# A fused attention and SwiGLU program whose order, engines and buffers stand in three tables: all three tables replaced

## The chip, the core and the metric

The program runs on one core of one Trainium2 chip. Its time is device microseconds (us), the median of three runs. The engines are PE (TensorE, matrix products), DVE (VectorE), ACT (ScalarE), POOL (GpSimd) and SP (SyncE, which here only issues DMAs). Each takes its instructions in the order in which the program holds them, and waits on semaphores for the others.

## The reference

Causal attention over 4 batches, 8 heads, 768 positions and 64 dimensions, in which heads 0, 2 and 6 see all earlier keys and the other five only the first 4 keys and a window of 64. Its output, as 3072 tokens of 512, goes through a SwiGLU block with 1536 hidden columns.

```python
scores = scale * np.matmul(q, k.transpose(0, 1, 3, 2))
stream_keep = causal & (is_sink | in_win)
mask = np.where(retr[0, :, 0, 0, None, None], full_mask, stream_mask)
scores = np.where(mask[None, :, :, :], scores, -1000000000.0)
scores = scores - np.max(scores, axis=-1, keepdims=True)
a = np.exp(scores)
a = a / (np.sum(a, axis=-1, keepdims=True) + 1e-09)
attn_out = np.matmul(a, v)
x = attn_out.transpose(0, 2, 1, 3).reshape(B * S, H * D)
g = x @ w_gate
silu = g * (1.0 / (1.0 + np.exp(-g)))
val = x @ w_val
out = silu * val @ w_out
```

## The kernel before

The work is cut into some 1060 **tasks**, and a task has a name by which the texts below call it. The 24 tiles of 128 queries (two to a pair, 12 pairs, numbered in the order of `TILES`) and the six groups of four tiles (512 tokens) of the SwiGLU block are the two counts on which names are built.

- `load q3`, `load k3`, `load x3`: DMAs of a pair's queries, keys and values, issued by SP (lines 349 and 354). `load g0`, `v0`, `o0` and so on are the sixths of the three weight matrices, 512 KB each (lines 360 and 362). They land in 11 `raw` buffers. `cq`, `ck`, `cx` and `wc` are the casts from there to 16 bits (lines 206, 208 and 212: the same copy on ACT, on POOL or DVE, and DVE's other form).
- `trq`, `trk` on PE and `evq`, `evk` turn the first five pairs' queries and keys (lines 473 and 208/206); from pair 5 on DMA transposes do it (`dq`, `dk`, line 463).
- `sc7.0` is the first unit of tile 7's scores on PE (line 567, up to eight products over 64 rows), `ex7.0` its exponentials on ACT (line 579), `mask7.0` the product with a 0/1 mask on DVE or POOL (line 587; unit 0 has 1024 columns, unit 1 has 640), `val7.1` and `val7.0` the products with the values on PE (line 597), `nm7` the division on DVE (a RECIPROCAL at line 604 and a TENSOR_TENSOR into `xb` at line 605). `sk` and `sv` are small copies of the first keys and values into later tiles' places.
- `xtr`, `xe` (tiles 0 to 7) or `xdma` (a DMA transpose by SP, line 615) put the tile's result into `xt`, the transposed input of its group.
- `gate2.8.0` and `vals2.8.0` are group 2's products for hidden block 8 (four matmuls each, line 759); `tanh` on ACT (line 765), `stt1` (line 769) and `stt2` (line 775) on DVE make the hidden activations `h_sb`. Group 0's first four blocks are halved, and the half's first column ends the name (0 or 256).
- The output projection of groups 0 to 4 uses seven products in place of eight: `out1.p1` to `out1.p7` on PE (line 839, twelve matmuls each), fed by sums of activations `hs` (line 826) and of weights `ws` (line 412) and gathered by `oe1.c11`, `oe1.r6` and so on, nearly all on DVE (line 855). Group 5 is projected plainly (`out5.0.0` and on, line 793). `st` are the stores.

PSUM has eight banks. A score unit or a tile's values take two neighbouring ones, a gate, vals or out product one, and PE may only write a bank when the reader of what stood there before (`ex`, `nm`, `stt1`, `stt2`, `oe`) is done.

No scheduler decides anything at run time or at build time. `ORDER` lists the tasks, two base-62 digits each, and the program is emitted in that order, so that each engine's queue is the list's part that falls to it; entries from 3700 up are fillers, some matmuls that keep PE going. `WAYS` has a digit for each task, the engine among those allowed, and `SLOTS` a digit for each buffer or bank that a task takes. `Plan.order` reads them:

Of the kernel before, what the change touches and what calls it, by code (L numbers as in the profile page):

```python
# [13 lines left out]


ORDER = (
    "0306071W091U1V1X000A08xy1c0D0C01050B1d1e040gy01f1gzJ1i1h2021282922232B1j1r1s021p1q1w0F2C2D2E2F1b"
    "2A2L2M2N2O2X2f2g0m1Y1a1Z1t1u1v1k0h252h1l1m2W2c242G2H2I2d2e2l2m2i2j0G271n1o1y1z3C262P2Q2R0z2t3031"
    "2J0y8e8o2n2K102U2o2p3I3J2V8t8j8m8u8v8k8l8n1x2k8f8g8p8q2x382y8h8i118r8s8w8x138y8z9893909495999A33"
    "340n9D9E0E2Z3K3D3L3M3N149B9C9F969G9H972a9192322b2Y2q2r2s2u3R3S3W3X0k1C9c9d9e9h9i9j3U3V3O2z353P36"  # L20
    "39370q1D9f9g9k9l3T3b3i3n3o3f3g0H3H3E3F2v2w0i169I9J9K9N9O9P0o179L9Q9R9M0l1F3Q3Y3Z3c3j3a0I3u40410j"
    "193k3h9m9n9o3l3m3A3B9S9T9U9r9s9t3d3e9X0J3v4344453G3p3q3r0r1G9u9p9v429Y9Z3s3t0x1H2S4647494A4H0p1A"
    "9V9WB74N4O4Q4R0K3z9q9zA10N4c3x4BB4B5B6B8Ak4K4L4V4b4C4D3yAT484M0w0sAQARASAU9a9b9y0t1E0W6K2TAlAmAV"
    "AWAX151M1O1N1PAYAZBEAfAgAhB9BABB4a0u181Q1R1SBCBDAp0v1BBFBGA0AaAbAnAoAc3wBHBIAdAe0L0M0PB20T12A41I"
    "1J1K0S4d4P0O4Z4h4g4Y4e4f5D5L5K0RAzB0B1AqArB31L0YALAM0ZAN4E4F4G4J4I6J1TAuAvAOAPAw9wA2A69xA3A7A55C"
    "5I5JAA4l4m4i4j4kACA8A9ABAD4n4v51524y53AiAj5f5lAEBMAGAFAK4S4z504T4W4UAxAy5g5nAsAtBL4q4r4o4p54BO0c"
    "AHAIAJ4s554t4u4x4wBJBKBQ56575T5U6MBNBP5W5c5XBb5j0X58595A5B707S7T6xBVBW6wBRBS5i5VBXBYBc6z5YBZBaBd"
    "5p5qBT5s605t5u4XBsBtBuCeCbCcCdCfCMCNCOCCBvBwCDCE0V6I5v0Q5F5G5H6v5k5o5M5N5O0UBiBjBk5rCPCQBlBm5E5Z"
    "5a5b5d5wCHCICJCWCXCY5m63696A666768Bh5h73CKCLC7C8C9710eCRCS5P5Q5R6465CACBCTBUC2C36y7Q6P74BnBo5x5y"
    "5z610a72CZCaBp5S625e6H6NBqBrC46B6C6F6D6GCFCGCiBeBfBgBxByBz7O7UC0C1C5C681CUCVCjCl6E6U6V6W6X6Y6R6S"  # L30
    "6T6eDmDjDkDlDnDoDpDqDrDs0b7P7X7WDtDuDv6Z6aCgChCn6b6c6d6fDUDVDWDXDY7576776g7C7D7E7F7G7L0dDwDxCkCm"
    "DSDFDGDHDPDQDRDT7b7c7d6QDADBDCDyDzE0DDDE7H80D5D6D7CsCt6O6n6o6h6i6j6kE1E27V7I7J7M7K7ND8D96l6m7879"
    "7A7BCoCpCrCuCv897Y7Z6p6q8786DKDLDMDZDaDb6L6r6s6t6uDcDdDeDfDgCwCx7e7f7R7j7m7n7o7p7q7rDNDOCyCzD0D4"
    "EhEiEjErEsEcEd88EkElEtCqD1D2D3EuEvEeDhDi7a7g7h7k7iFLFMFNFOFP7x8D8E8A8I8B8C8F8JFJFGFHFIFKFBFCFDDI"
    "DJE5E77s7t8GFEFFEp7u7v7y7w8HEXEYEZ0f838485EmEnEoEqEfEg8NEw8Y8ZE6E88T8U8VEzExEyF0EBE3E9E4EAECEDF6"
    "828K8L8M8OF1F2F3F9EFEG8Q8R8S8W8XEVEHEIEJF7F8FA7l8P7z8a8b8cEaEbESETEUEWEEEOELEM8dGiGMGTGUEKGCENER"
    "G7GVGWGjGkGJGKEPGREQFTFVGXGLGOGPGEGFGNGQG9F4GAGSGGGYGbGZF5GaGcGBGDFSGHFpFqFrFQFRG4G5GdGeFzFUFeFW"
    "FXGIG6G0G8FcFdGfFfFuFvFYFaFbGgGhG1G2G3FsFtFxGlGmFZFwFyFlFiFjFmFnFgFhFkFoGnGoGpGsGtGuGvGwGqGrGxGy"
    "GzH0H2H3H4H5H7H1H6H8H9"
)  # L40
WAYS = (
    "000010000000000000000000000000000000000000000000000000000000221202202202212200200111000111110010"
    "222200001100000000000000220022122022001011000000000000001100212002000011001001000001000001001000"
    "000201021120001000001001000000010010000010000000002221220000000000010000002000100100000020000221"
    "000000000100000002000010010000000000020200000010000000000000110000011000000100100000020001000000"
    "002202200220000000000000000012000100100000000201120000000000000000010002202202010000001001000001"
    "200000000000011002021000000000000000000200000000000000000000000000000000000000000000000000000000"
    "000000000000000000000000000000000000000000001000000000000000000000000000000000000000000000000000"
    "000000000000000000000000000000001000000010000000000000000000000000000000000000000000000000000000"
    "000000000000000000001110100011000000000001000000000000000000000000000000000000000000000000000000"  # L50
    "000000001111000001100000000000100000000000000000000000000000000000000000000000000000000000000111"
    "101100110000000000011000000000000000000000000000000000000000000000000000000000000000010000100000"
    "00000010"
)
# [965 lines left out]
```

## Time and profile before

| what | us |
| --- | --- |
| device time, median of 3 runs | 246.05 (245.79 to 246.59) |
| span of the profiled execution, first to last instruction | 244.4 |
| PE, DVE, ACT, POOL busy in it | 234.5, 186.7, 148.5, 129.0 |
| PE waiting for another engine or a DMA, longest in one place | 1.4 |

The profile gives no device time of its own for the profiled execution, only its span; the median of the three runs lies 1.65 us above that span. The profile is one execution. In its rows a number in square brackets behind an instruction is the idle time of its engine ahead of it, with who ended it; "x12" is a count; pieces of the chain of waits have a start and a duration, in us from the span's start.

### The profile page before, as it was taken

Reading aid. Unit: us, or ns where it says so; the run is one execution under the profiler, and the core shown is the slowest. Engines: PE = TensorE matmul, PEld = TensorE weight load, DVE = VectorE, ACT = ScalarE, POOL = GpSimd, SP = SyncE. Lnnn points to the kernel's source line nnn. Section 1 sums busy time; section 2 is a strip of 40 time slices with the busy share of each in tenths; the row PEclk is TensorE's granted clock in tenths of the full one; section 3 lists DMA queues with packets and bytes.
Section 4 is the critical chain, followed back from the end, with each engine's and each line's share of the span. In section 5 each row is a group of like instructions: output and inputs, shape, how many; then the busy total and the mean of one; then the engine's idle time right before and its main releaser. Section 6 shows DMA issues by size and latency. Waiting matters only on the chain.

```text
span 244.4 us, 5604 instructions
## 1 busy us (share of the span) xinstructions
PE 234.5 (96%) x2189; PEld 143.6 (59%) x2189; DVE 186.7 (76%) x324; ACT 148.5 (61%) x235; POOL 129.0 (53%) x140
## 2 busy tenths in 40 slices
...
GB/s 187 355 348 353 323 352 366 313 362 305 206 131 78 287 165 289 191 268 192 89 130 130 97 120 38 90 36 234 38 4 0 46 21 115 59 0 1 7 203 136
DMA packets 66794, 40.73 MB, mean 167 GB/s; under 512 B 25168, under 2 KB 60240, under 8 KB 66768
## 3 DMA queue, kind: packets, MB, share of 16 engines
...
q14 instruction: 9, 0.07, 0.1%
...
## 4 chain that ended last, share of the span: by engine, by line
PE 54%; DVE 19%; issue 8%; DMA 6%; POOL 5%; SPq 5%; ACT 2%; DVEq 0%; POOLq 0%
PE banks L759 34%; PE banks L839 10%; PE banks L793 4%; DMA raw<-in_moe_w_val_dram 4%; DVE h_sb L775 4%; PE banks L567 3%; DVE h_sb L826 3%; SPq L349 3%; DVE sil L769 3%; PE banks L597 2%; POOL hs_sb L826 2%; DVE out_sb L855 2%; DVE xb L605 2%; DMA xt<-xb 2%; DVE e L587 2%
## 5 line engine op out<-in xcount | busy, mean ns | idle before, releaser
L759 PE MATMUL banks<-xt,wg_sb 128*128 128x512 f16 (+1 forms) x304 | 70.3, 368 | 1.9 <-DMA xt<-xb 1.4
L759 PE MATMUL banks<-xt,wv_sb 128*128 128x512 f16 (+1 forms) x304 | 70.4, 368 | 0.8 <-DVE sil L769 0.7
L579 ACT ACTIVATE e<-banks 128x1024 f16<-128x1024 f32 (+2 forms) x68 | 58.7, 910 | 20.0 <-PE banks L567 11.7
L765 ACT ACTIVATE sig<-banks 128x512 f32<-128x512 f32 (+1 forms) x76 | 43.0, 577 | 43.5 <-PE banks L759 37.5
L769 DVE SCALAR_TENSOR_TENSOR sil<-sig,banks 128x512 f32<-128x512 f32 (+1 forms) x76 | 49.0, 656 | 14.8 <-ACT sig L765 12.6
L775 DVE SCALAR_TENSOR_TENSOR h_sb<-sil,banks 128x512 f16<-128x512 f32 (+1 forms) x76 | 48.7, 656 | 6.7 <-PE banks L759 4.4
L587 POOL TENSOR_TENSOR e<-e,m 128x640 f16<-128x640 f16 (+1 forms) x22 | 37.8, 1727 | 27.2 <-ACT e L579 24.3
L759 PEld LDWEIGHTS <-wg_sb 128*128 128x128 f16 x304 | 28.5, 98 | 30.7 <-issue 3.1
L759 PEld LDWEIGHTS <-wv_sb 128*128 128x128 f16 x304 | 28.2, 98 | 29.5 <-issue 1.2
L839 PEld LDWEIGHTS <-h_sb 128*128 128x128 f16 x360 | 34.8, 98 | 7.9 <-issue 0.7
L826 POOL TENSOR_TENSOR hs_sb<-h_sb 128x768 f16<-128x768 f16 x7 | 11.5, 1640 | 40.9 <-DVE h_sb L775 29.4
L855 DVE TENSOR_TENSOR out_sb<-banks,out_sb 128x512 f32<-128x512 f32 x35 | 23.6, 685 | 4.7 <-PE banks L839 4.4
L826 POOL TENSOR_TENSOR h_sb<-h_sb 128x768 f16<-128x768 f16 x11 | 18.0, 1639 | 8.2 <-PE banks L839 4.4
L839 PE MATMUL banks<-wo_sb,h_sb 128*128 128x256 f16 x180 | 21.9, 273 | 0.0
L839 PE MATMUL banks<-wt_sb,h_sb 128*128 128x256 f16 x180 | 21.5, 273 | 0.4 <-DVE out_sb L855 0.4
L567 PE MATMUL banks<-qT,kT 64*128 64x128 f16 x472 | 20.6, 218 | 1.1 <-DVE xb L605 1.0
L567 PEld LDWEIGHTS <-kT 64*128 64x128 f16 x472 | 14.6, 94 | 11.0 <-issue 10.2
L597 PEld LDWEIGHTS <-e 128*128 128x128 f16 x472 | 17.1, 97 | 4.3 <-ACT vt L206 0.9
L597 PE MATMUL banks<-vt,e 128*128 128x65 f16 x472 | 18.2, 193 | 1.0 <-POOL vt L208 0.7
L605 DVE TENSOR_TENSOR xb<-banks,rc 128x512 f16<-128x512 f32 x24 | 16.6, 691 | 0.8
L208 POOL CAST vt<-raw 64x512 f16<-64x512 f32 x22 | 14.4, 654 | 4.8 <-DMA raw<-in_v_dram 2.3
L206 ACT COPY out_sb<-banks 128x512 f32<-128x512 f32 (+1 forms) x7 | 4.0, 570 | 19.1 <-PE banks L793 16.0
...
## 6 DMA issues: line engine op xcount, KB each, us to landing
...
```

What stands on the lines that cost most here:

```text
L567: nc.tensor.matmul(sc[:, c:c + n, :], weights, moving, start=first, stop=last)
L579: nc.scalar.activation(out=to, in_=src, func=AF.Exp, scale=scale)
L587: ENG[task().way].tensor_tensor(out=ev, in0=ev, in1=mm, op=ALU.mult)
L597: nc.tensor.matmul(avs[t][:, odd, n * 66:n * 66 + 65], ee, vv, start=(m == 0), stop=(m == len(bl) - 1))
L605: nc.vector.tensor_tensor(out=xb.rearrange("p n o d -> p o n d"), in0=av[:, :, :, 0:64], in1=rc.to_broadcast([128, 2, 4, 64]), op=ALU.mult)
L759: nc.tensor.matmul(ps, wsb[:, kk, j * 128:(j + 1) * 128], xt[:, kk, c[0]:c[1]], start=(kk == 0), stop=(kk == 3))
L765: nc.scalar.activation(out=sg[g, j, c], in_=gs[g, j, c], func=AF.Tanh, scale=0.5)
L769: nc.vector.scalar_tensor_tensor(out=sl[g, j, c], in0=sg.pop((g, j, c)), scalar=1.0, op0=ALU.add, in1=gs.pop((g, j, c)), op1=ALU.mult)
L775: nc.vector.scalar_tensor_tensor(out=hs[g, j][:, c[0]:c[1]], in0=sl.pop((g, j, c)), scalar=0.5, op0=ALU.mult, in1=vs.pop((g, j, c)), op1=A ...
L826: ENG[T_hs[g, x][part].way].tensor_tensor(out=to, in0=a, in1=b, op=op)
L839: nc.tensor.matmul(rooms[g, p][:, x], left[:, j, 128 * x:128 * x + 128], right[:, j], start=(j == 0), stop=(j == NK - 1))
L855: nc.vector.tensor_tensor(out=cell(*to), in0=rooms[g, p], in1=cell(*other), op=ALU.add)
```

## The change

Only the three tables differ. Every task, its arithmetic and its shapes are the same, and so is the number of fillers (11 matmuls in three places, placed differently). The first line of each table, before and after:

```diff
 ORDER = (
-    "0306071W091U1V1X000A08xy1c0D0C01050B1d1e040gy01f1gzJ1i1h2021282922232B1j1r1s021p1q1w0F2C2D2E2F1b"
+    "060207xl0009030A08011U1V0D041W1X0C1c1f1dyE0B1g201h1i210g1e2822231j1r05292B0m1s1p0h2C1a2A1Z2D2E0E"
...
 WAYS = (
-    "000010000000000000000000000000000000000000000000000000000000221202202212202200200111000111110010"
+    "000010000000000000000000000000000000000000000000000000000000222222002202222220011011011110111012"
...
 SLOTS = (
-    "0014237653916A152371476981504A39A2564807049A28352A9168410016041002241601230163620442561014104122"
+    "101423105745851125376045A37912261A7446230143026693A470201012001302241602011043423044540401320063"
```

Decoded, the engines of these tasks change (tasks of a kind on ACT / DVE / POOL):

| kind | before | after |
| --- | --- | --- |
| casts of queries and keys, `cq` `ck` | 12 / 3 / 13 | 8 / 4 / 16 |
| casts of values, `cx` | 16 / 10 / 22 | 15 / 7 / 26 |
| first keys and values, `sk` `sv` | 14 / 8 / 10 | 7 / 7 / 18 |
| weights, `wc` | 6 / 2 / 12 | 5 / 1 / 14 |
| masks | - / 16 / 22 | - / 20 / 18 |
| sums, `hs` and `ws` | - / 23 / 29 | - / 21 / 31 |

On PE, scores stand in 31 separate runs where they stood in 32. Three places of the new order follow.

**SP, around the transposes of group 2's input.** These are SP's rows around the DMA transposes of tiles 10, 11 and 9 into the `xt` of group 2 (line 615; `xb_1598` is tile 10, `xb_1695` tile 11, `xb_1517` tile 9; line 354 are loads, 861 a store). Before:

```order
L463 DMA_TRANSPOSE kT0_104<-hq_1526 128x8x64
L354 DMA raw_1555<-in_v_dram 128x8x128
L861 DMA out_0_dram<-out_sb_94 128x2x512
L615 DMA_TRANSPOSE xt_1343<-xb_1598 128x4x128
L354 DMA raw_1665<-in_q_dram 128x8x128
L615 DMA_TRANSPOSE xt_1343<-xb_1695 128x4x128
L615 DMA_TRANSPOSE xt_1343<-xb_1517 128x4x128
L354 DMA raw_1831<-in_k_dram 128x8x128
```

And now, where `xb_1615` is tile 10, `xb_1382` tile 9 and `xb_1731` tile 11:

```order
L463 DMA_TRANSPOSE qT0_106<-hq_1465 128x8x64
L861 DMA out_0_dram<-out_sb_94 128x2x512
L463 DMA_TRANSPOSE qT1_107<-hq_1378 128x8x64
L615 DMA_TRANSPOSE xt_1421<-xb_1615 128x4x128
L354 DMA raw_1659<-in_v_dram 128x8x128
L615 DMA_TRANSPOSE xt_1421<-xb_1382 128x4x128
L615 DMA_TRANSPOSE xt_1421<-xb_1731 128x4x128
L354 DMA raw_1750<-in_q_dram 128x8x128
```

Tile 9 moved ahead of tile 11, which comes last; the load in front of tile 11's transpose is now one ahead of both.

**DVE, between the norms of tiles 3 and 5.** DVE's rows in the first gates of group 0 (L769 is `stt1`, L775 `stt2`, both in halves here; L587 a mask). Before:

```order
L775 SCALAR_TENSOR_TENSOR h_sb_92<-sil_534,banks_87 128x256
L769 SCALAR_TENSOR_TENSOR sil_542<-sig_540,banks_87 128x256
L769 SCALAR_TENSOR_TENSOR sil_546<-sig_544,banks_87 128x256
L212 TENSOR_REDUCE kT0_104<-kT0_104 128x2x2x2
L212 TENSOR_REDUCE kT0_104<-kT0_104 64x2x2
L775 SCALAR_TENSOR_TENSOR h_sb_92<-sil_542,banks_87 128x256
L775 SCALAR_TENSOR_TENSOR h_sb_92<-sil_546,banks_87 128x256
L775 SCALAR_TENSOR_TENSOR h_sb_92<-sil_530,banks_87 128x256
```

And now:

```order
L775 SCALAR_TENSOR_TENSOR h_sb_92<-sil_509,banks_87 128x256
L587 TENSOR_TENSOR e_468<-e_468,m1_102 128x1024
L769 SCALAR_TENSOR_TENSOR sil_583<-sig_572,banks_87 128x256
L769 SCALAR_TENSOR_TENSOR sil_589<-sig_566,banks_87 128x256
L775 SCALAR_TENSOR_TENSOR h_sb_92<-sil_542,banks_87 128x256
L769 SCALAR_TENSOR_TENSOR sil_610<-sig_593,banks_87 128x256
L775 SCALAR_TENSOR_TENSOR h_sb_92<-sil_583,banks_87 128x256
L587 TENSOR_TENSOR e_517<-e_517,m2_103 128x640
```

Masks of tiles 4 to 7, of which seven of eight stood in POOL's queue, are now all in DVE's.

**DVE, at the norm of tile 16.** L826 is a sum `hs` for group 2, L604 and L605 the norm. Before:

```order
L769 SCALAR_TENSOR_TENSOR sil_2212<-sig_2210,banks_87 128x512
L826 TENSOR_TENSOR h_sb_92<-hs_sb_93,h_sb_92 128x3x256
L604 RECIPROCAL rc_2259<-banks_87 128x8
L605 TENSOR_TENSOR xb_2258<-banks_87,rc_2259 128x2x4x64
L769 SCALAR_TENSOR_TENSOR sil_2270<-sig_2268,banks_87 128x512
```

And now:

```order
L769 SCALAR_TENSOR_TENSOR sil_2203<-sig_2196,banks_87 128x512
L604 RECIPROCAL rc_2227<-banks_87 128x8
L605 TENSOR_TENSOR xb_2226<-banks_87,rc_2227 128x2x4x64
L769 SCALAR_TENSOR_TENSOR sil_2242<-sig_2237,banks_87 128x512
L775 SCALAR_TENSOR_TENSOR h_sb_92<-sil_2203,banks_87 128x512
L769 SCALAR_TENSOR_TENSOR sil_2261<-sig_2256,banks_87 128x512
L769 SCALAR_TENSOR_TENSOR sil_2305<-sig_2301,banks_87 128x512
L212 TENSOR_REDUCE kT1_105<-kT1_105 128x2x2x2
L212 TENSOR_REDUCE kT1_105<-kT1_105 64x2x2
L826 TENSOR_TENSOR h_sb_92<-hs_sb_93,h_sb_92 128x3x256
```

The sum stood just ahead of the norm and stands eight rows behind it.

More of the change, by code (lines that the diff above doesn't have):

```diff
@@ L22 @@
[L22 to L36, printed above, removed]
@@ L37 @@
-    "G7GVGWGjGkGJGKEPGREQFTFVGXGLGOGPGEGFGNGQG9F4GAGSGGGYGbGZF5GaGcGBGDFSGHFpFqFrFQFRG4G5GdGeFzFUFeFW"
-    "FXGIG6G0G8FcFdGfFfFuFvFYFaFbGgGhG1G2G3FsFtFxGlGmFZFwFyFlFiFjFmFnFgFhFkFoGnGoGpGsGtGuGvGwGqGrGxGy"
-    "GzH0H2H3H4H5H7H1H6H8H9"
+    "060207xl0009030A08011U1V0D041W1X0C1c1f1dyE0B1g201h1i210g1e2822231j1r05292B0m1s1p0h2C1a2A1Z2D2E0E"
+    "1q1Y2X2L2F1b1w2f2M2W2N2g1t2O2h0F1u2S1k1l2c1v2425yG0n262d1m0G2G2H272e2l2I2i2m0z1n1y1o2P0y2Q1z2j0k"
+    "2J2t2R8o112o308p2K2p2U1x8q0q8r312V8e102x8f33138g8j340H2b8t8m0i388s8u9D8k2k2y3C988l8h8v0o998w8i2Y"
@@ new lines @@
+    "3I149A938n2Z0l328y949B3D958z963J8x9G900j9E3L2n1C97913M9C2q922r3K0I2a9c2s3N2u3R9F9d3W2z9h0v3X1D3S"
+    "9H359e369i3U3O0J37399k3P3b3F9j9f3V169l0p3H3i3l3E3f173j9N9g0r3g3Q2v9I3T9O3k3Y0x191F2w3Z9P9Q0s2T0t"
+    "3u9L9R9J3a9m3m0w3h400M9n9X9o0u3v3d9K9Y3n9S3c3G3o0K9M419r1A3e42439Z9T1B3p3q9s9U0P449a3r45469b1G49"
+    "3s4H123A9V9t4A3t9u3B479WB99v15484N4C4KBA9p4D0TBB1I4Q9qAQ4R0N1E4OBCAuAR1M0Q1H4L1NAV181J3yAfBD0L4P"
+    "ATAg9z3wAhAi0R3xASAzAWAj4Z9wA10W4BAv4MAxAUA3AX4E0S4FB4AwB01KB1B2B50O4G1QAY4YB3AL9y5G4eA44bAM4c1L"
@@ new lines @@
+    "B64hAkAyA0AZ4gBEAlAN9xAO1R4f3z1O4IAnBF5g0XAP5h4S4T0YA21TAa5DA5ApBG5f5L1S4UA84W5lAm1PAA4VA9Aq4JAo"
+    "4lAr4i5nAs4j4vAB4aAC5CAt5KA76v4mB75JA6ADAb4q540bBHAc555o4k4rAE4dBI5IB86w4o514yAF4pAH4n52BLAGAd53"
+    "AIAK4sAJAe4t4z5mBZ4uBM4x5W565T5k5XBOBJ0Z4w575c4XBNBRBK505UBP5859BQ5i5VBVBU5H5ABX5BBW5j0U5Y5v5MBY"
+    "Bb0c5NBS0V5EBa5w745p5sBTBcCM5t0eCbCN5u0a5F6MBdCH5O6H5q5ZCO5aCKCICcCJ6z6OBs5dCLCPBtCd606ICeBu5rCQ"
+    "Bv6PCfBi5b6QBw6366Bj6981646NBkBl67CC65Bm6E5P5x5Q5y6A5RBnCD5SC2BoCE68Be735z616Z6UBh6aCF5e6VBf6BCG"
@@ new lines @@
+    "6C7S62BxBp6FC36DC00fBy6J70Bz6G6X6R7PC4C56S0dC16WCW71C6C76y7W6TBqC86YC9CA72CXBrCRCY7O7XCZCS6x6KCT"
+    "CU88CiCBDjCa6bCVDkDmCkDl6cDo6d6eCjDyDp6g7TDqCgDzDn7UClE07F7C75ChBg7GDP7VCmD5DQ76DRE17LD6DrCn777D"
+    "E2DtDs6LDwD7857RDuDADv7ECsDBDxDC7b6k6hCt7c80DD6l7H78DUDE6i7I8479DX7ADV6f7JDWDK6jDYD8DL7KDeDM6m6n"
+    "6pD97Y866qDS836oCo7QDT897M7d6rDf7NCp6s7ZDF7j6t7B7aDNDgDGDH6uDZDO7e7p7m7qCw7f7nDI7g7oCu7hCvCyCrDJ"
+    "CxErCzE6EcD07iD4FGEd7xDaEeDcCqDbEsEuDdFH82Dh7kEt7r8G7s7lDi8HF1EvE887FID1F27tF38DE58A8ID28BF4FJ8N"
@@ L40 @@
+    "F58C8E7u7v8JFB7wE78Y8TFKFC7zEa8ZFD8U7yD3EXE38FEYEZ8KE48LFE8M8OEBEA8PFFESECE98Q8W8V8REDEFET8XEhEG"
+    "8SEUEVEbFL8aFM8bEiFNF98cEfEW8dEmEjEJEgEnEwELFOF6FPEoEpF7ExF8EzEqG4FAEkG5GHElEEEHG6FTGJEyEIFuGKF0"
+    "GCFvEKGEFVEMG7GLFxGFG8FwEOENFSERGMG9GNEPFQGAEQGBGdFzGeFRGfFYFyFUGOFXFWGgGPGQGRGDG0FaFpGSG2FZFbGh"
+    "FcG1G3FqGWFdFiFrGGGTGYGUGVFlFeFsFfGlFjFmGiGIFnFgGjGXGZFtGbGkGaGnGmGoGcFhGpFkGsGqFoGtGrGuGxGvGyGw"
+    "GzH2H0H3H1H4H7H5H6H8H9"
 )
 WAYS = (
-    "000010000000000000000000000000000000000000000000000000000000221202202202212200200111000111110010"
@@ L43 @@
[L43 to L52, printed above, removed]
@@ L53 @@
-    "00000010"
+    "000010000000000000000000000000000000000000000000000000000000222222002202222220011011011110111012"
+    "122101101100000000000000110022122022010011000000000000001200222221000011000000000001100000000000"
+    "001100221210000000000000000000001000000000000000002200200000000010000000000000000000000220002102"
+    "000000000000000001100000010000000000221000000000000000001000010002022000000100000000100001000000"
+    "002102020000000001001000000011000100100000000122220000000100000010010000202222000000001001000001"
@@ new lines @@
+    "200010010000010022222000000010000000000210001000000000000000000000000000000000000000000000000000"
+    "000000000000000000000000000000000000000000101001001100000000000010000000000000000000000000000000"
+    "000000000000000000000000000000001000000110000000000000000000000000000000000000000000000000000000"
+    "000000000000000000001111100011000000000000000000000000000000000000000000000000000000000000000000"
+    "000000001011100001000000000000100000000000000000000000000000000000000000000000000000000000000000"
@@ L54 @@
+    "001000110000000000001000000000000000000000000000000000000000000000000000000000000000110001100000"
+    "00000001"
 )
 SLOTS = (
-    "0014237653916A152371476981504A39A2564807049A28352A9168410016041002241601230163620442561014104122"
-    "636011642065221025144416322211256461406003404624344620616540610143626540604164236062324342142254"
-    "041614064616325426212246140636104325614261306242452460436460636014122636230644521206164434062601"
-    "020211341120003102001134000210400214105510131201001011040122021303213020111113411111040020200051"
```

13 lines of the change are left out of this document (6 added, 7 removed).

## The prediction

> **What bounds the kernel now.** I read the page's busy times first:
>
> ```profile
> span 244.4 us, 5604 instructions
> ...
> PE 234.5 (96%) x2189; PEld 143.6 (59%) x2189; DVE 186.7 (76%) x324; ACT 148.5 (61%) x235; POOL 129.0 (53%) x140
> ```
>
> PE is not busy for 9.9 us of the span. To see whether its busy time is work or hides slow stretches, I took the last stage out of the chain of waits (start, duration, what):
>
> ```profile
> 200.24 13.81 PE banks L759 x64
> ...
> 227.06 3.93 PE banks L839 x36
> 230.99 10.40 PE banks L793 x60
> ```
>
> 64 gate and vals matmuls in 13.81 us are 0.216 us each, a gate or vals task (four) 0.86; an `out` product of twelve is 1.31. PE runs without a gap here, and nothing in the tables can shorten these matmuls. **PE is the bound**, so the change can win only what PE waits. The timeline of PE shows where (idle time ahead in brackets, and who ended it):
>
> ```profile
> 1.36 4.69 PE L321 MATMUL banks<-ident 128*128 128x512 f16 x12 [1.36 <-POOL ident L234]
> ...
> 17.75 0.42 PE L597 MATMUL banks<-vt,e 128*128 128x65 f16 x8 [0.71 <-POOL vt L208]
> ...
> 56.59 1.02 PE L759 MATMUL banks<-xt,wg_sb 128*128 128x512 f16 x4 [0.45 <-DVE sil L769]
> ...
> 59.60 1.02 PE L759 MATMUL banks<-xt,wv_sb 128*128 128x512 f16 x4 [0.25 <-DVE sil L769]
> ...
> 82.35 1.47 PE L839 MATMUL banks<-wt_sb,hs_sb 128*128 128x256 f16 x12 [0.18 <-DVE out_sb L855]
> ...
> 91.00 0.83 PE L567 MATMUL banks<-qT,kT 64*128 64x128 f16 x22 [0.44 <-DVE xb L605]
> ...
> 136.75 0.85 PE L567 MATMUL banks<-qT,kT 64*128 64x128 f16 x24 [0.51 <-DVE xb L605]
> ...
> 188.95 1.47 PE L839 MATMUL banks<-wt_sb,h_sb 128*128 128x256 f16 x12 [0.45 <-DVE out_sb L855]
> ...
> 191.40 1.02 PE L759 MATMUL banks<-xt,wv_sb 128*128 128x512 f16 x4 [0.43 <-DVE sil L769]
> ```
>
> and PE's waits by who ended them have one more, the longest:
>
> ```profile
> PE banks L759 <- DMA xt<-xb: 1.4, 1, 1.4
> ```
>
> 1.36 us come before the first matmul and about 3.0 after the last (230.99 + 10.40 = 241.4); the other 5.5 are spread in small waits, most of them ended by DVE. That is the whole prize, 2% of the time. Beyond PE, DVE is close behind in the middle, as the windows view shows (PE, PEld, DVE, ACT and POOL busy, in us):
>
> ```profile
> 21.00:49.00 28.00, 27.87 (x328) 18.50 (x326) 23.00 (x50) 25.82 (x46) 26.93 (x28) 1.00 1.10 341
> 56.00:98.00 42.00, 40.58 (x394) 27.32 (x393) 40.72 (x68) 32.40 (x48) 24.75 (x22) 1.00 0.91 204
> ```
>
> DVE works 40.72 of 42 us between 56 and 98; between 21 and 49 it has 5 us to spare, and POOL 1.
>
> **The change part by part.** The sum is made on the span and carried to the median: 246.05 plus the difference. Differences within 0.3% (0.74 us) count as no change; about that much is what measuring this kernel can tell.
>
> *One score run fewer: -0.2.* A run of scores pays at its ends beyond its matmuls:
>
> ```profile
> 24.11 0.33 PE banks L567 x8
> ...
> 111.92 0.77 PE banks L567 x22
> ```
>
> Eight in 0.33 and 22 in 0.77 give 0.031 each and 0.08 at the entry; the exit isn't shown, and I allow 0 to 0.3.
>
> *The start: -0.5.* The 0.71 us wait at 17.75, for a value cast, sits behind exponentials that now start earlier: the fillers ahead of the first scores are moved in front of the data. But the fourth sixth of the gate weights is the sixteenth load in both orders, and its cast and the gate that needs it are these rows:
>
> ```profile
> 30.08 1.03 POOL L208 CAST wg_sb<-raw 128x1024 f16<-128x1024 f32 x1
> ...
> 31.03 0.51 PE L567 MATMUL banks<-qT,kT 64*128 64x128 f16 x11
> 31.47 0.82 PE L759 MATMUL banks<-xt,wg_sb 128*128 128x512 f16 x3
> ```
>
> That gate now stands ahead of the two score units at 31.03, worth 0.44 us. It can't come before the cast, which ends at 31.1 and could end earlier only if POOL took it sooner. Whatever is won before 30 us is capped there: between 0 and 1.0, and I take half.
>
> *Seven masks from POOL to DVE, tiles 4 to 7: +0.7.* One mask on either engine:
>
> ```profile
> L587 POOL TENSOR_TENSOR e<-e,m 128x1024 f16<-128x1024 f16 x10 | 21.2, 2122 | 8.3 <-ACT e L579 5.3 <-PE banks L597 3.0
> L587 POOL TENSOR_TENSOR e<-e,m 128x640 f16<-128x640 f16 x12 | 16.7, 1397 | 19.0 <-ACT e L579 19.0
> L587 DVE TENSOR_TENSOR e<-e,m x16: 482/678/1360, 44.5 to 191.9; 128x1024 f16<-128x1024 f16 x10, 128x640 f16<-128x640 f16 x6
> ```
>
> (The last gives the least, middle and longest duration.) POOL sheds 3 x 2.12 + 4 x 1.40 = 12.0 us; DVE gets 3 x 0.68 + 4 x 0.48 = 4.0. Against that, DVE sheds casts and small copies there and takes others:
>
> ```profile
> L212 DVE TENSOR_REDUCE vt<-raw 64x512 f16<-64x512 f32 x10 | 6.8, 680 | 0.3
> L212 DVE TENSOR_REDUCE vt<-vt 2x330 f16<-2x330 f16 x8 | 3.8, 481 | 0.1
> L208 DVE COPY xt<-banks 128x512 f16<-128x512 f16 x6 | 2.4, 419 | 0.1
> L208 DVE COPY qT<-banks 128x512 f16<-128x512 f16 x2 | 1.4, 683 | 0.0
> ```
>
> One `cx`, one `evq`, `wc v0.0` (0.7 each) and `sv0.2`, `sv0.4` (two of 0.48 each) go, two `cx` and an `xe` (0.4) come: -4.0 + 1.8. Net +1.8, so DVE has 24.8 of 28 us, 3.2 to spare. If it stays so, PE waits no longer. What speaks against it is how DVE's masks and sums last beside POOL's work. DVE, then POOL:
>
> ```profile
> 57.59 1.36 DVE L587 TENSOR_TENSOR e<-e,m 128x1024 f16<-128x1024 f16 x1
> ...
> 78.16 0.55 DVE L826 TENSOR_TENSOR h_sb<-hs_sb,h_sb 128x768 f16<-128x768 f16 x1
> 78.75 1.75 DVE L826 TENSOR_TENSOR h_sb<-h_sb 128x768 f16<-128x768 f16 x1
> ```
>
> ```profile
> 78.68 1.39 POOL L587 TENSOR_TENSOR e<-e,m 128x640 f16<-128x640 f16 x1 [1.45 <-ACT e L579]
> ```
>
> The same sum takes 0.55 us alone and 1.75 when POOL had begun a mask 0.07 us before it: it ends 0.43 after POOL does. So a mask put on DVE waits for what POOL is at. Eight such waits have 3.2 us to hide in: the threshold is 0.4 us each. Their size isn't shown for casts as long as 1.03; bounds are 0 and 1.2 (1.75 - 0.55), so 0 to +6.4 on PE. I take 0.49, nearest to the 0.68 of the mask at 57.59 (1.36 - 0.68) but shortened because POOL, 12 us lighter, is at rest part of the time: 8 x 0.49 - 3.2 = +0.7.
>
> *The middle: -0.4.* The 0.44 at 91.00 is tile 11's scores waiting for the bank that `nm10` frees, with one `out` product (1.31) between. Now `out1.p4` and `sc13.1` stand between, 1.31 + 0.33, so 0.33 goes, and no gather stands directly ahead of that norm: all 0.44, between 0 and 0.44. The three other waits for DVE (0.45, 0.25, 0.18) stay, since DVE's tasks there hardly change.
>
> *Group 2's input: -1.1.* The 1.4 us wait:
>
> ```profile
> 95.15 3.18 SPq L615 DMA_TRANSPOSE xt<-xb  x2
> ```
>
> ```profile
> 94.19 0.22 DVE rc L604
> ...
> 94.44 0.69 DVE xb L605
> ...
> 96.40 4.70 DMA xt<-xb
> ```
>
> SP stood at tile 11's transpose until its norm ended at 95.13; tile 9's, ready long before, was queued behind it and landed last, at 101.1 (96.40 + 4.70). The order's rows above now put tile 9 first, so one transpose is left after the norm. PE's cover, from `val11.0` to the first gate, was four `out` products and two score units; it is now three products and four units, 3 x 1.31 + 27 x 0.031 plus entries, about 5.0 us. Needed are the norm (0.22 + 0.69) and a landing, which is bounded by this view of line 615:
>
> ```profile
> DMA to landing us min/median/max: 2.4/2.7/5.8
> ```
>
> 3.3 to 6.7 against 5.0: a wait of 0 to 1.7, and I take 0.3, as one transpose instead of two is left.
>
> *From 100 us on: -0.5.* At 136.75 the norm of tile 16 came after a sum that lasted long, and two gates (1.72) covered it. Now the sum stands behind the norm and the cover is two gates and a product, 3.0: 0.51 goes. At 191.40 `vals4.0.0` waited for an `stt1`; its bank is now freed by an exponential 2.2 us of PE work earlier: 0.43 goes. The 0.45 at 188.95 stays, since `out3.p6` has just 1.5 us after `out3.p2`. For a new order's own waits I add one of the mean of the three, 0.46. Bounds -1.4 to +0.5.
>
> *The end: +0.2.* `vals5.9.0` now stands directly ahead of the last projection, whose third part needs its `stt2`. DVE's tasks there last as in these rows:
>
> ```profile
> L775 DVE SCALAR_TENSOR_TENSOR h_sb<-sil,banks 128x512 f16<-128x512 f32 (+1 forms) x76 | 48.7, 656 | 6.7 <-PE banks L759 4.4
> ...
> L855 DVE TENSOR_TENSOR out_sb<-banks,out_sb 128x512 f32<-128x512 f32 x35 | 23.6, 685 | 4.7 <-PE banks L839 4.4
> ```
>
> From the end of `out4.p7` on, DVE has three gathers and three `stt2` queued (4.0), then two `stt1` and two `stt2` (2.6): 6.6 us. PE has three gate or vals tasks (2.6), `out4.p4`, `vals5.9.0` and eight matmuls (1.3 + 0.9 + 1.7): 6.5. So 0.1 and a hand-over or two, between 0 and 0.6.
>
> Sum: -0.2 - 0.5 + 0.7 - 0.4 - 1.1 - 0.5 + 0.2 = -1.8, a span of 242.6, **244.2 us**.
>
> **A rule against it.** The Trainium skill ("SBUF — State Buffer", section "SBUF: two separate sides") says that VectorE and GpSimd share one port pair as an exclusive lock, held for a whole instruction: a VectorE operation with two SBUF inputs blocks fully until GpSimd's is over. The pair of rows at 78.7 agrees. By it, a mask meeting a cast at a random point would wait half the cast, 0.5, when POOL is busy, and by an estimate 0.4 on the mean, POOL being at work 22 of the 28 us (26.9 less 12.0, and some 7 of casts and copies that come to it); the third term would be 0 and the time 243.5, still inside the forecast's case.
>
> **The rivals.** (1) *The DVE masks wait for POOL much longer.* Same place, 22 to 49 us. At 0.9 each it is 8 x 0.9 - 3.2 = 4.0 in place of 0.7: +1.5, **247.5**. It turns the result's sign from 0.71 each on (8 x 0.71 - 3.2 = 2.5, all the other terms together). For it: 1.75 and 1.36 above. Against it: POOL's casts are shorter than its masks. (2) *The waits move.* DVE, full from 56 to 98, gives back in new places what is gone at 91, 101 and 137 (0.44 + 1.1 + 0.5): **246.2**. For it: 40.72 of 42. Against it: the longest wait is a DMA's and not DVE's. (3) *The waits after 50 us all go*: 0.45 + 0.25 + 0.18 + 0.44 + 1.4 + 0.51 + 0.45 + 0.43 = 4.1, with the other terms -0.2 - 0.5 + 0.7 - 4.1 + 0.2 = -3.9, **242.2**. For it: where I compared the cover of a wait, at 91, 101, 137 and 191, it was long enough or nearly. Against it: DVE's 40.72 of 42. (4) *The tables don't do it*: emission follows `ORDER` literally, so this is left out.
>
> **How the numbers follow.** The forecast's case (243.0 to 245.3) 0.42; rival 3 and better, under 243.0, 0.14; rival 2, within 0.74 of before, 0.19; rival 1, 0.25. Faster 0.56, same 0.19, slower 0.25. The range goes from 241.6, rival 3 with the start's other half, to 248.0, rival 1 with 0.96 each; about 0.07 is left out below and 0.12 above.
>
> **What would show it.** PE's wait for `xt` under 0.6; no idle time ahead of the scores after `val16.0`; the first full gate of block 8 before 31.2; DVE masks between 22 and 49 us with a mean under 1.1 us, and PE busy 27 of those 28 us. It is wrong if those masks average over 1.3, if POOL's casts come late for the gates, or if PE's idle time after 56 us is still over 4 us.

## The result and the profile after

| | before | after |
| --- | --- | --- |
| device time, median (range), first measurement | 245.95 (245.79 to 246.59), 4 runs | 244.20 (243.46 to 245.04), 4 runs |
| the same, second measurement | 246.09 (245.24 to 247.01), 23 runs | 245.23 (243.27 to 245.72), 12 runs |
| ratio to before, 95% interval | | 0.9931 [0.9904, 0.9957], then 0.9950 [0.9929, 0.9970] |
| span of the profiled execution | 244.4 | 243.1 |

The kernel became faster by 0.5 to 0.7%. The first measurement meets the forecast of 244.2; the second shows a gain of 0.9 us where 1.8 was forecast. The profile shows that this sum came about in another way than I had worked it out. The page's first lines, as of before:

```profile
span 243.1 us, 5586 instructions
...
PE 235.2 (97%) x2189; PEld 144.1 (59%) x2189; DVE 182.7 (75%) x324; ACT 137.0 (56%) x212; POOL 140.8 (58%) x163
```

PE's waits by line and who ended them (in all, how often, the longest), complete:

```profile
PE banks L839 <- DVE out_sb L855: 2.5, 1, 2.5
PE banks L321 <- POOL ident L234: 1.4, 1, 1.4
PE banks L473 <- ACT e L579: 0.4, 1, 0.4
PE banks L759 <- POOL wv_sb L208: 0.3, 1, 0.3
PE banks L473 <- DVE hq L212: 0.2, 1, 0.2
```

Of the waits that the prediction listed only the first matmul's 1.4 is left; the three of 0.2 to 0.4, all before 22 us, are not in its list. In place of the others stands one wait of 2.5 us which before did not have. The windows view shows where (PE, PEld, DVE, ACT, POOL busy, then the granted clock, the DMA share and GB/s):

```profile
21.00:49.00 28.00, 27.63 (x334) 18.17 (x332) 24.22 (x52) 23.74 (x41) 20.48 (x29) 1.00 1.09 359
56.00:98.00 42.00, 39.50 (x376) 26.06 (x375) 38.76 (x63) 28.17 (x41) 27.88 (x26) 0.96 0.98 215
98.00:140.00 42.00, 41.97 (x378) 23.60 (x376) 32.94 (x58) 27.41 (x43) 32.99 (x32) 1.00 0.90 182
140.00:190.00 50.00, 49.95 (x513) 31.38 (x511) 35.88 (x63) 26.76 (x41) 34.38 (x31) 1.00 0.20 49
```

From 98 to 190 us PE idles for less than 0.1 us. Between 56 and 98 it idles for 2.50 us, and the clock granted there is 0.96 on the mean. Its timeline has both in one row, the first two products of group 0 that use the sums:

```profile
76.96 4.45 PE L839 MATMUL banks<-wt_sb,h_sb 128*128 128x256 f16 x24 [2.50 <-DVE out_sb L855]
```

24 matmuls take 4.45 us, where the same two products take 2.78 in each of the next four kernels. So this place costs 2.50 + 1.67 = 4.17 us in this execution. The 1.67 are a stretch of 3.41 us at half the clock, with the full clock before and after it, as the windows view shows:

```profile
74.39:77.80 3.41, 0.91 (x9) 0.85 (x9) 3.38 (x5) 1.62 (x5) 1.50 (x2) 1.00 1.03 214
77.80:81.21 3.41, 3.41 (x18) 2.29 (x16) 3.12 (x5) 0.60 (x1) 0.00 (x0) 0.50 1.17 213
81.21:84.62 3.41, 3.41 (x37) 2.33 (x36) 2.34 (x3) 2.59 (x3) 2.57 (x5) 1.00 0.45 75
```

`out0.p6` waits for the bank of `out0.p2`, which the gather `oe0.c11` on DVE frees. It also multiplies with what the sum `hs0.2.0` makes, as PE's weight loads show:

```profile
76.36 0.10 PEld L839 LDWEIGHTS <-h_sb 128*128 128x128 f16 x1 [2.39 <-DVE h_sb L826]
```

PE had ended its last gate at 74.46, so without the gather some 1.9 of the 2.50 would be left (76.36 - 74.46, an estimate). DVE's timeline, then POOL's, at that time:

```profile
71.92 0.69 DVE L775 SCALAR_TENSOR_TENSOR h_sb<-sil,banks 128x512 f16<-128x512 f32 x1
72.53 3.78 DVE L826 TENSOR_TENSOR h_sb<-hs_sb,h_sb 128x768 f16<-128x768 f16 x1
76.23 0.68 DVE L855 TENSOR_TENSOR out_sb<-banks,out_sb 128x512 f32<-128x512 f32 x1
```

```profile
71.95 0.60 POOL L208 CAST vt<-raw 64x512 f16<-64x512 f32 x1
72.52 1.15 POOL L412 TENSOR_TENSOR wt_sb<-wo_sb,wt_sb 128x512 f16<-128x512 f16 x1
73.64 1.14 POOL L412 TENSOR_TENSOR wt_sb<-wo_sb 128x512 f16<-128x512 f16 x1
74.75 1.14 POOL L412 TENSOR_TENSOR wt_sb<-wo_sb,wt_sb 128x512 f16<-128x512 f16 x1
```

The sum `hs0.2.0`, 0.55 us alone, lasts 3.78: it ends (76.31) 0.42 after the last of three weight sums that POOL runs back to back (`ws4.2`, `ws3.2`, `ws4.1`). The gather stands behind it, and PE behind both.

### The profile page after: what moved, and what is told of

Same layout as the page of the kernel before. It is cut to its first block, busy times and chain, and to the rows that moved or that the text cites. A ratio compares the mean times of both kernels' runs of the same rounds, so it can differ in the third digit from the quotient of the medians.

```text
span 243.1 us, 5586 instructions
## 1 busy us (share of the span) xinstructions
PE 235.2 (97%) x2189; PEld 144.1 (59%) x2189; DVE 182.7 (75%) x324; ACT 137.0 (56%) x212; POOL 140.8 (58%) x163
## 2 busy tenths in 40 slices
DMA packets 66793, 40.72 MB, mean 168 GB/s; under 512 B 25168, under 2 KB 60240, under 8 KB 66768
## 3 DMA queue, kind: packets, MB, share of 16 engines
q10 hardware_dynamic: 1248, 2.16, 2.7%
## 4 chain that ended last, share of the span: by engine, by line
PE 78%; DVE 8%; DMA 6%; issue 3%; SPq 2%; ACT 1%; POOL 0%; DVEq 0%; ACTq 0%
PE banks L759 44%; PE banks L839 19%; PE banks L567 6%; PE banks L597 5%; PE banks L793 4%; DMA raw<-in_v_dram 4%; DVE sil L769 2%; DMA raw<-in_k_dram 2%; DVE h_sb L775 2%; SPq L362 2%; DVE vt L212 1%; PE banks L473 1%; DVE xb L605 1%; DVE e L587 1%; ACT sig L765 0%
## 5 line engine op out<-in xcount | busy, mean ns | idle before, releaser
L579 ACT ACTIVATE e<-banks 128x1024 f16<-128x1024 f32 (+2 forms) x68 | 59.6, 911 | 25.4 <-PE banks L567 22.6
L759 PE MATMUL banks<-xt,wg_sb 128*128 128x512 f16 (+1 forms) x304 | 71.7, 368 | 0.0
L769 DVE SCALAR_TENSOR_TENSOR sil<-sig,banks 128x512 f32<-128x512 f32 (+1 forms) x76 | 48.9, 655 | 16.2 <-ACT sig L765 15.1
L775 DVE SCALAR_TENSOR_TENSOR h_sb<-sil,banks 128x512 f16<-128x512 f32 (+1 forms) x76 | 48.5, 654 | 10.9 <-PE banks L759 8.8
L839 PEld LDWEIGHTS <-h_sb 128*128 128x128 f16 x360 | 35.5, 100 | 11.8 <-DVE h_sb L826 2.4
L587 POOL TENSOR_TENSOR e<-e,m 128x1024 f16<-128x1024 f16 (+1 forms) x18 | 33.5, 1864 | 10.0 <-ACT e L579 9.6
L839 PE MATMUL banks<-wt_sb,h_sb 128*128 128x256 f16 x180 | 23.5, 286 | 2.5 <-DVE out_sb L855 2.5
L826 POOL TENSOR_TENSOR h_sb<-h_sb 128x768 f16<-128x768 f16 x14 | 23.3, 1668 | 4.0 <-PE banks L567 2.6
L826 POOL TENSOR_TENSOR h_sb<-hs_sb,h_sb 128x768 f16<-128x768 f16 x3 | 5.1, 1701 | 32.1 <-DVE h_sb L826 27.5
L208 POOL CAST hq<-raw 128x1024 f16<-128x1024 f32 (+1 forms) x16 | 14.9, 934 | 7.5 <-DMA raw<-in_q_dram 2.6
L208 POOL CAST vt<-raw 64x512 f16<-64x512 f32 x26 | 16.6, 640 | 2.4 <-DMA raw<-in_v_dram 1.1
L605 DVE TENSOR_TENSOR xb<-banks,rc 128x512 f16<-128x512 f32 x24 | 16.6, 692 | 0.8
```

The costliest lines, as they stand in the source:

```text
L208: ENG[task.way].tensor_copy(out=dst, in_=src)
L579: nc.scalar.activation(out=to, in_=src, func=AF.Exp, scale=scale)
L587: ENG[task().way].tensor_tensor(out=ev, in0=ev, in1=mm, op=ALU.mult)
L759: nc.tensor.matmul(ps, wsb[:, kk, j * 128:(j + 1) * 128], xt[:, kk, c[0]:c[1]], start=(kk == 0), stop=(kk == 3))
L769: nc.vector.scalar_tensor_tensor(out=sl[g, j, c], in0=sg.pop((g, j, c)), scalar=1.0, op0=ALU.add, in1=gs.pop((g, j, c)), op1=ALU.mult)
L775: nc.vector.scalar_tensor_tensor(out=hs[g, j][:, c[0]:c[1]], in0=sl.pop((g, j, c)), scalar=0.5, op0=ALU.mult, in1=vs.pop((g, j, c)), op1=A ...
```

## The experiments

Two theories were set against each other first. **A**: DVE's sum is shut out while POOL goes on with two-input instructions, and the rest follows. **B**: the sum is late for a reason of its own. Four kernels change only the neighbourhood of `hs0.2.0`; in the diffs the tables are decoded to task names and engines.

**One weight sum left on POOL.**

```diff
-DVE:  hs0.2.0, oe0.c11, ..., stt1 1.5.0, oe0.r6
-POOL: ws4.2, ws3.2, ws4.1
+DVE:  hs0.2.0, oe0.c11, ..., stt1 1.5.0, ws4.2, ws4.1, oe0.r6
+POOL: ws3.2
```

> After, with two of the three weight sums that POOL runs beside hs0.2.0 (ws4.2, ws4.1) given to DVE, behind the gather oe0.c11, so that POOL has one (ws3.2, 1.14 us) there. Theory A (DVE's sum is kept out for as long as POOL goes on with two-input instructions, the gather that frees p6's bank stands behind it, and the 2.5 us idle PE then runs slower for some us): hs0.2.0 lasts about 1.6 us instead of 3.78, the wait ahead of out0.p6 is about 0.4 instead of 2.50, the two products take 2.7 instead of 4.45: 244.2 - 2.1 - 1.8 = 240.3 us, up to 241.5 if the two sums are in DVE's way (0.58 each). Theory B (the sum is late for a reason of its own, such as what it reads, and PE's slow stretch is not a result of the wait): hs0.2.0 lasts over 3 us still, 244.2 within 0.7.

**Two left.**

```diff
-DVE:  hs0.2.0, oe0.c11, ..., stt1 1.5.0, oe0.r6
-POOL: ws4.2, ws3.2, ws4.1
+DVE:  hs0.2.0, oe0.c11, ..., stt1 1.5.0, ws4.1, oe0.r6
+POOL: ws4.2, ws3.2
```

> As e1, but only ws4.1 goes to DVE and POOL keeps two sums (ws4.2, ws3.2) beside hs0.2.0. Theory A: hs0.2.0 ends 0.42 after the second, so it lasts 2.7 us, the wait ahead of out0.p6 is 1.4. If PE's slow stretch comes only from a long idle time (1.4 us did not bring it in before), the products take 2.7: 244.2 - 1.1 - 1.8 = 241.3. If any wait of over a microsecond brings it, 243.1. Theory B: 244.2 within 0.7.

**The sum itself on POOL.**

```diff
-DVE:  stt2 1.0.0, hs0.2.0, oe0.c11
-POOL: cx7.0.0, ws4.2, ws3.2, ws4.1
+DVE:  stt2 1.0.0, oe0.c11
+POOL: cx7.0.0, hs0.2.0, ws3.2, ws4.2, ws4.1
```

> After, with hs0.2.0 itself on POOL, ahead of the three weight sums, of which ws3.2 (which out0.p7 needs) now comes first. Theory A: hs0.2.0 takes 1.64 on POOL and ends at 74.2, ahead of the end of gate1.6.0 (74.46); DVE's gather oe0.c11 runs at once; no wait over 0.3 ahead of out0.p6 or p7, PE at full rate: 244.2 - 2.5 - 1.8 = 239.9 us (239.4 to 240.8). Theory B: 244.2 within 0.7.

**The sum two instructions earlier.**

```diff
-DVE:  ws2.2, sv1.2, stt2 1.0.0, hs0.2.0, oe0.c11
+DVE:  ws2.2, hs0.2.0, sv1.2, stt2 1.0.0, oe0.c11
```

> After, with hs0.2.0 earlier in DVE's queue by two instructions (ahead of sv1.2 and stt2 1.0.0), so that it asks at about 71.0, in the middle of POOL's ws3.1, behind which POOL has a cast (cx7.0.0, 0.6 us, one input) and the three sums. Theory A1 (DVE gets in as soon as POOL is at an instruction with one input): it ends at about 72.5, no wait ahead of out0.p6: about 240.2. Theory A2 (DVE is kept out until POOL has nothing more): it ends at 76.3 again and takes sv1.2 and stt2 1.0.0 with it (1.7 us): wait about 4, 246. Theory B: 244.2 within 0.7.

Measured, in us, with before at 246.34 on the chip of the four new kernels; the first row is the two measurements above:

| kernel | median (range) | ratio, 95% interval | `hs0.2.0` | wait of `out0.p6` | span |
| --- | --- | --- | --- | --- | --- |
| after, first and second measurement | 244.20, 245.23 | 0.9931, 0.9950 | 3.78 | 2.50 | 243.1, 242.6 |
| two left | 242.73 (242.70 to 243.33) | 0.9863 [0.9840, 0.9885] | 2.67 | 1.39 | 240.6 |
| one left | 242.58 (242.50 to 243.02) | 0.9853 [0.9835, 0.9870] | 1.57 | 0.29 | 240.3 |
| two earlier | 242.49 (242.42 to 243.22) | 0.9852 [0.9831, 0.9873] | 1.50 | none | 240.6 |
| on POOL | 241.62 (240.54 to 242.46) | 0.9807 [0.9768, 0.9847] | 1.64 | none | 238.9 |

DVE's sum, then POOL's weight sums, in the run with two left:

```profile
72.18 2.67 DVE L826 TENSOR_TENSOR h_sb<-hs_sb,h_sb 128x768 f16<-128x768 f16 x1
```

```profile
72.17 1.15 POOL L412 TENSOR_TENSOR wt_sb<-wo_sb,wt_sb 128x512 f16<-128x512 f16 x1
73.28 1.15 POOL L412 TENSOR_TENSOR wt_sb<-wo_sb 128x512 f16<-128x512 f16 x1
```

It ends at 74.85, and POOL's second at 74.43. With one left (`ws3.2` from 72.16 to 73.32) it ends at 73.74. So it ends 0.42 after the first, the second or the third, whichever is POOL's last: each weight sum more costs 1.1 us, and B falls. The run with the sum moved earlier shows when DVE gets in although POOL has more to do (DVE, then POOL):

```profile
70.55 1.50 DVE L826 TENSOR_TENSOR h_sb<-hs_sb,h_sb 128x768 f16<-128x768 f16 x1
```

```profile
70.28 1.36 POOL L412 TENSOR_TENSOR wt_sb<-wo_sb 128x512 f16<-128x512 f16 x1
71.58 0.93 POOL L208 CAST vt<-raw 64x512 f16<-64x512 f32 x1
72.48 1.15 POOL L412 TENSOR_TENSOR wt_sb<-wo_sb,wt_sb 128x512 f16<-128x512 f16 x1
```

It ends 0.41 after `ws3.1`, and the cast that comes next on POOL is 0.93 long instead of 0.60: where POOL's next instruction has one input, DVE's sum goes first and the cast waits (A1).

But two inputs on POOL do not always keep DVE out. In the profile of the changed kernel DVE's `ws2.2`, with two inputs, began while POOL ran `hs0.3.0`, and `ws3.1`, also with two inputs, stood right behind that (DVE, then POOL):

```profile
70.41 0.58 DVE L412 TENSOR_TENSOR wt_sb<-wo_sb,wt_sb 128x512 f16<-128x512 f16 x1
```

```profile
69.07 1.64 POOL L826 TENSOR_TENSOR h_sb<-h_sb 128x768 f16<-128x768 f16 x1
70.67 1.33 POOL L412 TENSOR_TENSOR wt_sb<-wo_sb 128x512 f16<-128x512 f16 x1
```

`ws2.2` ended 0.28 after `hs0.3.0`, and `ws3.1` took 1.33 instead of 1.15: here DVE went next. The profiles of all its variants show the same, with `ws2.2` at 0.58 to 0.60. So it is shown that the row of weight sums kept `hs0.2.0` out; what lets DVE in between two sums of POOL is open.

All four times lie above what theory A had for them: 242.73 for 241.3, 242.58 for 240.3 (up to 241.5), 242.49 for 240.2 and 241.62 for 239.9 (239.4 to 240.8). For one thing, I took 1.8 for the slow stretch off the median of 244.2, though three of the four executions behind it have a granted clock of 1.000; without that the four are 243.1, 242.1, 242.0 and 241.7. For another, new waits came. In the run with the sum earlier, `sv1.2`, now behind it, came late for the values of tile 9, and PE waited there, 1.3 us. With two and one left DVE's shift gave PE a wait at `sc10.0`, 0.46 and 0.79.

PE's two products take 2.78 us in all four profiles and the granted clock is 0.999 or 1.000 in every one of their 16 executions. So the slow stretch belongs to the wait of 2.5 us; one of 1.39 did not bring it.

**The changed kernel again, and two parts of the change alone.** The first run is the kernel itself. The second gives the masks back (seven ways of tiles 4 to 7), the third gives them to DVE in before, the fourth undoes two waits in before:

```diff
 second, in after
-mask4.0 mask4.1 mask5.0 mask5.1 mask6.0 mask6.1 mask7.1: DVE
+mask4.0 mask4.1 mask5.0 mask5.1 mask6.0 mask6.1 mask7.1: POOL
 third, in before
-mask4.0 mask4.1 mask5.0 mask5.1 mask6.0 mask6.1 mask7.1: POOL
+mask4.0 mask4.1 mask5.0 mask5.1 mask6.0 mask6.1 mask7.1: DVE
 fourth, in before
-SP:   xdma11, xdma9
+SP:   xdma9, xdma11
-DVE:  hs2.2.1, nm16
+DVE:  nm16, hs2.2.1
```

> The changed kernel as it is, on the chip of the next three runs. hs0.2.0 takes 3.8 us again and the wait ahead of out0.p6 is 2.5 again, if the order alone makes them; 244.2 (243.5 to 245.0), or 0.993 of before. On PE's slow stretch behind that wait: if an idle time of 2.5 us brings it each time, the granted clock is 0.993 in every run; if only at times (the first four runs had 0.993 once and 1.000 three times), most runs have 1.000 and a span about 1 us shorter, and the two products take 2.7 us in place of 4.45.

The wait was 2.49 and the products took 4.27 us in this profile too. Of the 12 executions nine had a granted clock of 0.993 (242.9 to 243.6 us of span in eight, 242.6 in the profiled one) and three of 1.000 (241.3 to 241.9). With the first four runs that is 10 of 16: the slow stretch, some 1.6 us, comes in some executions and not in others. The median of the first measurement had it once in four, that of the second nine times in twelve, and so they lie 1 us apart.

> After, with the seven masks of tiles 4 to 7 back on POOL, all else as it is. If the masks on DVE cost what the prediction put down (+0.7 us, DVE waiting 0.49 for POOL with each), the time falls to 243.5. If they cost nothing on DVE and POOL's room is what they bought, POOL has 20.5 + 12.0 = 32.5 us of work in the 28 us from 21 to 49 and runs late by up to 4.5: 246 to 249.

251.21 us (251.11 to 251.97), ratio 1.0216 [1.0190, 1.0242], 6 us over after: the direction was right and the size too low. PE is busy only 22.20 of the 28 us:

```profile
21.00:49.00 28.00, 22.20 (x249) 14.28 (x250) 15.31 (x34) 18.62 (x31) 26.81 (x30) 1.00 1.05 343
```

POOL is full, and PE waits for its masks (2.5 us), its casts of queries and keys (2.3) and of weights (0.5).

> Before, with the seven masks of tiles 4 to 7 on DVE, all else as it is: DVE then has 23.0 + 4.0 = 27.0 of the 28 us from 21 to 49. If a mask waits 0.49 for POOL, DVE is over by 7 x 0.49 - 1.0 = 2.4: 248.4. If masks are not slowed there, 246.0 within 0.7 and POOL falls to 15 busy us; if POOL's lateness was what PE waited for in that stretch, down to 245.

253.45 us (252.62 to 253.64), ratio 1.0297 [1.0271, 1.0323], 5 us beyond my worse case. Three rows of DVE's timeline there, then the casts of weights that POOL ran beside the first mask:

```profile
35.40 1.30 DVE L587 TENSOR_TENSOR e<-e,m 128x1024 f16<-128x1024 f16 x1
...
44.93 1.28 DVE L775 SCALAR_TENSOR_TENSOR h_sb<-sil,banks 128x512 f16<-128x512 f32 x2 [0.72 <-PE banks L759]
46.13 1.15 DVE L587 TENSOR_TENSOR e<-e,m 128x1024 f16<-128x1024 f16 x1
```

```profile
35.12 1.04 POOL L208 CAST wg_sb<-raw 128x1024 f16<-128x1024 f32 x1
36.10 1.50 POOL L208 CAST wv_sb<-raw 128x1024 f16<-128x1024 f32 x1
```

A mask that starts within a cast does end late (36.70, 0.54 after the first cast), and the next cast then waits for it (1.50 instead of 1.04). Four of the eight masks from 20 to 51 us met one so and lasted 2.1 us longer in all than the 0.48 or 0.68 of the others. But PE idles 6.2 of the 28 us from 21 to 49, and most of that is the place in the queue: the mask at 46.13, whose exponentials were done at 38.23, stood behind `stt2` that waited for PE, and PE then waited 2.45 us for it. The masks' engine and the order around them were chosen together, and neither engine takes the masks in the other's order.

> Before, with tile 9's transpose ahead of tile 11's in SP's queue, and hs2.2.1 behind the norm of tile 16 on DVE; nothing else. By the prediction's working: the 1.4 us wait of gate2.8.0 for xt falls to 0 to 0.3, and the 0.51 us wait of tile 18's scores goes: 246.0 - 1.1 - 0.5 = 244.4. If DVE gives them back in new places: the two waits are gone in the profile, others of the same sum come up behind them, and the time is 246.0 within 0.7.

245.50 us (244.24 to 246.41, 12 runs), ratio 0.9970 [0.9948, 0.9991]: 0.6 us, less than the 1.6 expected. The executions lie in two groups, six from 244.24 to 245.07, the profiled one among them, and six from 245.93 to 246.41, where nothing is gained; why was not traced. In the profile the sum's 0.51 is gone entirely, and of the transposes' 1.36 there remains

```profile
100.75 1.02 PE L759 MATMUL banks<-xt,wg_sb 128*128 128x512 f16 x4 [0.80 <-DVE out_sb L855]
```

The transposes now land at 100.61, only 0.49 earlier than the 101.10 of before, and a gather frees a bank at 100.74. So the order of SP's queue alone is worth 0.5 there and not 1.1. (This first gate is `gate2.2.0` in before's order, and not `gate2.8.0` as I wrote.)

**A second buffer.** The run with the sum on POOL had executions near 240.7 and near 242.4. In its profile the multiplication of tile 11's norm waited 0.83 us for tile 10's transpose, which still read the same `xb` buffer. The third buffer stood idle:

```diff
 the sum on POOL, one digit of SLOTS
-nm11: xb 2 (as nm10)
+nm11: xb 1
```

> e3_sum_on_pool, with the norm of tile 11 writing into the third xb buffer, idle since the start, instead of the one that tile 10's transpose is still reading (in e3 the multiplication at line 605 waited 0.83 us for that transpose to land, and gate2.8.0 then 0.2 for tile 11's). Theory X (the two times of e3, 240.5 to 240.9 and 242.4 to 242.5, differ by when tile 10's transpose lands, which nm11, then tile 11's transpose, then gate2.8.0 pass on): nm11 takes 0.9, tile 11's transpose lands 0.8 earlier, no wait ahead of gate2.8.0, and all runs lie near 240.5. Rival (the two times come from elsewhere): the waits go all the same, the median falls by 0.2 at most, and the runs still lie in two groups 1.6 us apart.

> e3_sum_on_pool once more beside e11, for its spread: runs near 240.7 and near 242.4 again. If the profiled run is one of the later ones, theory X expects a wait of 1.6 to 1.9 us ahead of gate2.8.0 in it, for tile 11's transpose; the rival expects it in another place.

With the own buffer 241.31 us (240.64 to 242.62, 6 runs), ratio 0.9821 [0.9791, 0.9851]; the sum on POOL again 242.08 (241.39 to 242.13, 4 runs), 0.9835 [0.9809, 0.9861]. The profile of the latter caught a late execution, DVE and then PE:

```profile
95.82 0.69 DVE L605 TENSOR_TENSOR xb<-banks,rc 128x512 f16<-128x512 f32 x1 [2.44 <-DMA xt<-xb]
```

```profile
96.56 0.49 PE L567 MATMUL banks<-qT,kT 64*128 64x128 f16 x11 [1.14 <-DVE xb L605]
```

Tile 10's transpose landed at 95.72 there and at 94.20 in the first profile; the norm and PE passed 1.1 us of it on, at `sc14.2` and not at `gate2.8.0` as expected. With its own buffer the norm ran without a wait (0.69 at 93.44). Tile 11's transpose landed no earlier for that (98.10, where theory X had it 0.8 earlier), since SP was busy with tile 9's until 95.02. The runs still spread over 2 us, and not in two clear groups, so neither theory came out as written: the shared buffer passed on a late landing in one profile, and what it adds to the spread is not shown. The intervals do not tell the two kernels apart. Both beat before and after.

## Why the prediction came out right

The time was right, but by luck: two large errors in it cancelled.

**The step that failed** is "for a new order's own waits I add one of the mean of the three, 0.46". The new order's own wait was 2.50 us, and a slow stretch of 1.67 came behind it in the profiled execution: 4.17. The mechanism stood in my own rows: at 78.7 a sum of DVE ended 0.43 after POOL's mask. I applied it to the masks of 21 to 49 us alone, and did not look for the other sums of DVE that the new order puts beside POOL's. `hs0.2.0` was one, with three weight sums beside it and, behind it, the product that needs it and the gather that frees the product's bank. Nor did I see that the price can multiply by POOL's back-to-back instructions.

**The terms that I mis-sized the other way** sum to nearly the same. Without that place the span would be 243.1 - 4.17 = 238.9, and the profiled execution with the sum on POOL has just that (all four go from 238.6 to 240.5). So all other terms are worth -5.5 there, and I had -2.3 without the 0.46. By the three executions without the slow stretch, 241.3 to 242.1 less 2.50, they are worth -4.8 to -5.6 (an estimate, as the wait was not profiled in these).

For the masks, this is DVE's group of them between 21 and 49 us (least, middle and longest duration in ns):

```profile
L587 DVE TENSOR_TENSOR e<-e,m x8: 476/678/724, 24.7 to 42.3; 128x1024 f16<-128x1024 f16 x4, 128x640 f16<-128x640 f16 x4
```

One of them began within the second of two casts of POOL (DVE, then POOL):

```profile
27.12 0.69 DVE L587 TENSOR_TENSOR e<-e,m 128x640 f16<-128x640 f16 x1
```

```profile
26.20 1.27 POOL L208 CAST vt<-raw 64x512 f16<-64x512 f32 x2
```

- *Start, -0.5*: `gate0.8.0` begins at 30.81 instead of 31.47, -0.66. Right: POOL took its cast sooner, which ended at 30.69 instead of 31.11.
- *Masks, +0.7*: nearly no cost. They take 0.48 or 0.68 by their size, and seven of the eight are within 0.05 of that: they start while POOL rests or copies, or just ahead of its casts, which then wait themselves (1.37 instead of 1.04 at 32.44). The one at 27.12 took 0.21 more. The 0.49 was between 0 and 1.2, and I took a value near the slow rows. PE is never idle from 31 to 56 us. The windows came out near what was worked out, DVE at 24.22 (24.8) and POOL at 20.48 (22). The sum by the Trainium skill ("SBUF — State Buffer", section "SBUF: two separate sides") had 0 for this term, but out of waits of 0.4 on the mean, which did not come. It gives the lock to whichever engine starts first, for the whole instruction, and does not say which comes next when it is free: the three profiles above show `hs0.2.0` last, and `ws2.2` at 70.41 next.
- *The middle, -0.4, and from 100 us on, -0.5*: 0.44, 0.51 and 0.43 went as argued. But the waits that I kept went too (0.45, 0.25 and 0.18 before 83 us, 0.45 at 188.95), since each of these tasks' banks is now free 0.3 to 1.0 us ahead of it: `gate1.1.0` at 54.00 finds its `stt1` done at 53.58, `out3.p6` at 181.90 its gather at 181.29. The first three I kept "since DVE's tasks there hardly change"; DVE's busy time from 56 to 98 fell from 40.72 to 38.76, and from 140 to 190 from 38.78 to 35.88, with POOL up from 23.03 to 34.38 there. Whether that relief or the places in the order freed them was not tried apart.
- *Group 2's input, -1.1*: the wait is gone, all 1.36. The reason was half right: SP's order alone brought 0.5 in before. PE's cover came out as worked out, 4.96 us from `val11.0` to the gate (97.29 to 102.25). The norm ended at 98.37, and the transpose landed 3.66 us after its issue instead of 5.47, at 102.05, just 0.2 ahead of the gate. Why it landed sooner is not shown; with 5.47 PE would have waited at least 1.6 us (98.39 + 5.47 = 103.86, an estimate), so this was luck in part.
- *The end, +0.2*: no wait. *One score run fewer, -0.2*: not seen by itself. PE's busy time without the slow stretch is 233.5 and was 234.5; 0.8 of that was not traced to a cause.

**The rivals.** The first did not happen. The masks on either engine in the other's order cost 6 to 7 us, but by its places in the queue and POOL's load in the main and not by the waits of this rival. The third, all waits after 50 us gone, is what happened, and the second, a new wait in place of the old ones, happened with it, in one place.
